# Backward pass of an attention block on one core: dW4 computed at the turn from the forward to the backward part, and two tiles used a second time

## The chip, the core and the metric

The kernel runs on one core of a Trainium2 chip. A core has TensorE (PE: matrix products into PSUM), VectorE (DVE), ScalarE (ACT), GpSimd (POOL) and SyncE (SP), each with an instruction queue of its own, and 16 DMA engines that move data between the chip's large memory (HBM) and the on-chip SBUF. Here SP issues almost all loads and POOL all stores. The metric is device time in microseconds, lower is better; a run without the profiler gives one time, and the kernel before is given by the median of three.

## What is computed

One token goes through a decoder block with a modulated layer norm, attention over a cache of 8192 positions for 32 heads of width 192, and a small MLP; wanted are the output and the gradients towards nine of the inputs. Cut to what matters here:

```python
def _A_ref(x, k_cache, v_cache, wq, wo):              # attention, one query row
    scores = jnp.einsum('bhqd,bhkd->bhqk', q, k) * Dh ** (-0.5)
    p = _softmax(scores, axis=-1)
    o = jnp.einsum('bhqk,bhkd->bhqd', p, v)
    return o.reshape(B, Sq, Hq * Dh) @ wo
def _fwd_reference(...):
    x = x + ga * _A_ref(h, A_k_cache, A_v_cache, A_wq, A_wo)
    h = _layernorm(x) * (1 + cb) + sb
    x = x + gb * _B_ref(h, B_w1, B_w2, B_w3, B_w4)    # ... gelu(layernorm(.) @ w3) @ w4
...
_out, _vjp = jax.vjp(_f, A_x, A_k_cache, A_v_cache, A_wq, A_wo, B_w3, B_w4, c, w_mod)
```

With a single token, every weight's gradient is an outer product of two vectors. For W4 (1536 x 640) it is the activation g = gelu(u), 1536 long, times the gradient at the MLP's output, 640 long: dW4[f, :] = g[f] * dbo[:]. For the V cache, dV of a head is the softmax row p times the gradient do of that head's output (8192 x 192), and dK is the same with dS and q. All data is bfloat16. K and V are read (V twice), dK and dV are written: about 100 MB each.

## The kernel before

**Forward part.** A loop over 32 heads streams K and V in half heads of 128 partitions x 32 rows x 192 (`JH` = 32; 1.5 MB each), forms scores, softmax and the products with V. The normalised exponentials (`E_all`) stay on chip.

**The turn.** After the last head, the rest of the forward part and the start of the backward part run as one chain of small steps in a column layout (a vector of 1536 lies as 128 x 12, its columns called f): layer norms, u = n2 W3, gelu, g (`g_f` in float32, `g_bf`), then du, dn2 = W3 du, two layer norm backward steps (`ln_bwd_cols`, "lb2" and "lb1"), dao, do of the last head pair (`do_bf`, spread over the partitions as `do_pb`). W3 and W4 sit in three of the five 1.5 MB tiles of the pool `big`: `w_t[0]` holds the first 512 rows of W3, `w_t[1]` the last 128 rows of W3 and 7 of 12 blocks of W4, `w_t[2]` the other 5 blocks of W4 and a rest of the transposed W3; a fourth, `w_t[3]`, holds the transposed W3, written block by block (`w3T_some`) and read by the dn2 matmuls (L764). `mid_mm` (matmuls of L798) computes g W4 from `w_t[1]` and `w_t[2]`. The fifth tile of the pool holds half of V of head 30.

`ln_bwd_cols` has a `fill` callback that is called between the matmul for the means and VectorE's use of its result. For "lb2" it transposes two blocks of wo (`woT_some(2)`), for "lb1" it is `lb1_fill` (one more block, the broadcast of q, and a copy).

**Backward part.** A loop over the heads from the last to the first (`HS`). For a head, `bwd_mult` multiplies V by do on VectorE and sums over the width on TensorE; `bwd_dv` makes dV for half a head: ScalarE makes the first `na` = 20 of 32 row blocks (L903), VectorE the other 12 (L880, `pairs_outer`), and POOL issues the store (L909). `bwd_ds` and `bwd_dk` make dK on VectorE, stored by L924. dV and dK take their tiles from `big`, in the order in which the pool's tiles come free. For the very first half (`bwd_dv(HS[0], 0, 0, 2)`) VectorE makes all 32 row blocks, in two pieces, each with its own store. V comes through a ring of six tiles and is loaded ahead as far as the ring allows.

Gradients of the weights are jobs attached to the heads of the loop (`J0`, `J1`, `J2`): `job_dwo` at heads 1 to 16, `job_dw4` at 17 to 20, `job_dw3` at 21 to 25, and larger jobs for wq and w_mod. `job_dw4(k)` makes three of twelve row blocks on ScalarE (`tsc` with k even, L939) in a tile of the pool `bso` (two tiles) and stores them with one DMA (L947). `job_dw3` multiplies on VectorE (L941).

The order of TensorE, VectorE and ScalarE is the order in which the instructions are written (`pin_order`); POOL's and SP's queues are ordered by the framework's scheduler, and all waits between engines are set by the framework from the tiles that are read and written.

Of the kernel before, what the change touches and what calls it, by code (L numbers as in the profile page):

```python
# [9 lines left out]
BF16 = mybir.dt.bfloat16  # L10
ALU = mybir.AluOpType
# [9 lines left out]
def kernel(  # L21
# [26 lines left out]
    nc = tc.nc  # L48
# [16 lines left out]
    P = 128  # L65
    D = A_x.shape[-1]
    _, HQ, S, DH = A_k_cache.shape
# [10 lines left out]
    HH = HQ // 2  # L78
# [6 lines left out]
    NAV = 40  # L85
# [8 lines left out]
    def bank(tag, bufs=1, name=None, n=512):  # L94
        return psum[0].tile([P, n], FP32, tag=tag, name=name or "ps_" + tag, bufs=bufs)
# [31 lines left out]
    def ccol(n, name, dtype=FP32):  # L127
        return const.tile([P, n], dtype, name=name)

    def mul(out, a, b):  # L130
        nc.vector.tensor_tensor(out=out, in0=a, in1=b, op=ALU.mult)  # L131

    def add(out, a, b):
        nc.vector.tensor_tensor(out=out, in0=a, in1=b, op=ALU.add)  # L134
# [4 lines left out]
    def stt(out, in0, scalar, in1, op0, op1):  # L139
        nc.vector.scalar_tensor_tensor(out=out, in0=in0, scalar=scalar, in1=in1, op0=op0, op1=op1)  # L140
# [6 lines left out]
    def neg_means(parts, n, name):  # L147
        ps = bank_c(name)
        nc.tensor.matmul(ps[:, 0:n], lhsT=negd_mat, rhs=parts, start=True, stop=True)
        return ps[:, 0:n]  # L150

    def ln_cols(x_c, pfx, fill=lambda k: None):
        s1 = ccol(1, pfx + "_s1")
        nc.vector.reduce_sum(out=s1, in_=x_c, axis=AX.X)
        m_ps = neg_means(s1, 1, pfx + "_m")
        fill(0)
        xc = ccol(NDC, pfx + "_xc")
        add(xc, x_c, m_ps.to_broadcast([P, NDC]))
        sq = ccol(NDC, pfx + "_sq")
        s2 = ccol(1, pfx + "_s2")  # L160
        nc.vector.tensor_tensor_reduce(out=sq, in0=xc, in1=xc, scale=1.0 / D, scalar=0.0, op0=ALU.mult, op1=ALU.add, accum_out=s2)
        v_ps = col_sums(s2, 1, pfx + "_v")
        std = ccol(1, pfx + "_std")
        nc.scalar.activation(out=std, in_=v_ps, func=ACT.Sqrt, bias=eps_c[:, 0:1], scale=1.0)
        rstd = ccol(1, pfx + "_rstd")
        nc.vector.reciprocal(out=rstd, in_=std)
        fill(1)
        nrm = ccol(NDC, pfx + "_n")
        nc.vector.tensor_scalar(out=nrm, in0=xc, scalar1=rstd[:, 0:1], scalar2=None, op0=ALU.mult)
        return nrm, rstd  # L170

    def ln_bwd_cols(dn, n, rstd, add_to, out, pfx, fill=lambda: None):
        s = ccol(2, pfx + "_s")
        nc.vector.reduce_sum(out=s[:, 0:1], in_=dn, axis=AX.X)
        jk = ccol(NDC, pfx + "_jk")
        nc.vector.tensor_tensor_reduce(out=jk, in0=dn, in1=n, scale=1.0, scalar=0.0, op0=ALU.mult, op1=ALU.add, accum_out=s[:, 1:2])
        m_ps = neg_means(s, 2, pfx + "_m")
        fill()
        t = ccol(NDC, pfx + "_t")
        mul(t, n, m_ps[:, 1:2].to_broadcast([P, NDC]))  # L180
        add(t, t, dn)
        add(t, t, m_ps[:, 0:1].to_broadcast([P, NDC]))
        stt(out, t, rstd[:, 0:1], add_to, ALU.mult, ALU.add)

    def bcast_cols(col_bf, c0, n, out_bc, evac, ps_in=None):
        for g0 in range(0, n, 4):
            g1 = min(n, g0 + 4)
            ps = ps_in if ps_in is not None else bank_c("bc_ps")
            for k in range(g0, g1):
                nc.tensor.matmul(ps[:, (k - g0) * P : (k - g0 + 1) * P], lhsT=col_bf[:, c0 + k : c0 + k + 1].to_broadcast([P, P]), rhs=ident_bf, start=True, stop=True)  # L190
            evac(out_bc[:, g0 * P : g1 * P], ps[:, 0 : (g1 - g0) * P])
# [4 lines left out]
    def dve_copy(out, in_):  # L196
        nc.vector.tensor_copy(out=out, in_=in_)
# [26 lines left out]
    def big_tile(name):  # L224
        return big.tile([P, JH, DH], BF16, name=name, tag="big")
# [84 lines left out]
    dbo_c = ccol(NDC, "dbo_c")  # L310
# [3 lines left out]
    dbo_bc = const.tile([P, D], BF16, name="dbo_bc")  # L314
# [24 lines left out]
    def pair_bc(pool, col_bf, hp, name, ps=None):  # L339
        t = pool.tile([P, 2 * DH], BF16, name=name, tag=name)  # L340
        bcast_cols(col_bf, 3 * hp, 3, t, act_copy, ps)
        return t
# [152 lines left out]
    def flat(tl):  # L495
        return tl.rearrange("p j d -> p (j d)")
# [48 lines left out]
    for i in range(1, HQ + 2):  # L545
        if i == HQ + 1:
            nc.scalar.activation(out=warm, in_=eps_c, func=ACT.Sqrt)
        c, p, pp = 2 <= i < HQ, 0 <= i - 1 < HQ, 0 <= i - 2 < HQ
        n = i + 1 < HQ
# [5 lines left out]
        if i == HQ - 1:  # L555
            w_t = [flat(big_tile(f"w_t{k}")) for k in range(2)]
# [78 lines left out]
    def woT_some(n):  # L635
        for g in range(woT_next[0], min(woT_next[0] + n, 4)):
            t_ps = bank("s", 2, "t_ps", SB[0])
            blks = range(4 * g, min(4 * g + 4, 3 * NDC))
            for k, blk in enumerate(blks):
                nc.tensor.matmul(t_ps[:, k * P : (k + 1) * P], lhsT=woT[:, blk * P : (blk + 1) * P], rhs=ident_bf, start=True, stop=True)  # L640
            nc.scalar.copy(out=woT[:, 512 * g : 512 * g + P * len(blks)], in_=t_ps[:, 0 : P * len(blks)])
        woT_next[0] += n
# [20 lines left out]
    bso = ctx.enter_context(tc.tile_pool(name="bso", bufs=2, reuse_waits="tile"))  # L663
    bsm = ctx.enter_context(tc.tile_pool(name="bsmall", bufs=2, reuse_waits="tile"))
    HS = list(range(HQ - 1, -1, -1))
# [35 lines left out]
    st2 = nc.gpsimd  # L701
# [27 lines left out]
    n2_c, r2 = ln_cols(hb_c, "ln2", lambda k: w3T_some(k + 1))  # L729
# [27 lines left out]
    g_f = ccol(NFC, "g_f")  # L757
    mul(g_f, u, sg)
    g_bf = ccol(NFC, "g_bf", BF16)
    dve_copy(g_bf, g_f)  # L760
    dn2_ps = bank("b")
    for i in range(NDC):
        for f in range(NFC):
# [3 lines left out]
    dn2 = ccol(NDC, "dn2")  # L767
    dve_copy(dn2, dn2_ps[:, 0:NDC])
    dhb = ccol(NDC, "dhb")
    ln_bwd_cols(dn2, n2_c, r2, dbo_c, dhb, "lb2", lambda: woT_some(2))  # L770
    def lb1_fill():
        woT_some(1)
        q_pb[PS[0]] = pair_bc(bsm, q_bf, PS[0], "q_pb")
        nc.scalar.copy(out=kb_sb, in_=kb_ps[:, 0 : 2 * DH])

    dn1 = ccol(NDC, "dn1")
    mul(dn1, dhb, cb1)
    dx1 = ccol(NDC, "dx1")
    ln_bwd_cols(dn1, n1_c, r1, dy_c, dx1, "lb1", lb1_fill)
    dao_bf = ccol(NDC, "dao_bf", BF16)  # L780
    mul(dao_bf, dx1, ga)
# [104 lines left out]
    def vec_of(d, h):  # L886
        return d[h // 2][:, (h % 2) * DH : (h % 2 + 1) * DH]
# [7 lines left out]
            nc.tensor.matmul(bst[h]["dP_ps"][:, t * JH : (t + 1) * JH, :], lhsT=ident_bf, rhs=V_sb[:, :, k * DS : (k + 1) * DS], start=(k == 0), stop=(k == NDS - 1))  # L895
        freed.add(("v", h, t))

    def bwd_dv(h, t, na=NAV // 2, parts=1):
        o = big_tile("dV")
        j0 = t * JH  # L900
        doh = vec_of(do_pb, h)
        for jj in range(na):
            nc.scalar.activation(out=o[:, jj, :], in_=doh, func=ACT.Copy, scale=bst[h]["PF"][:, j0 + jj : j0 + jj + 1])  # L903
        n = JH // parts
        for r0 in range(0, JH, n):
            r1 = r0 + n
            ra = max(r0, na)
            pairs_outer(o[:, ra:r1, :], bst[h]["P2h"][:, j0 + ra : j0 + r1, :], doh, r1 - ra)
            st2.dma_start(out=dV_hd[h][:, j0 + r0 : j0 + r1, :], in_=o[:, r0:r1, :])  # L909
# [27 lines left out]
    def tsc(out, in_, col, k):  # L937
        if k % 2 == 0:
            nc.scalar.activation(out=out, in_=in_, func=ACT.Copy, scale=col)  # L939
        else:  # L940
            nc.vector.tensor_scalar(out=out, in0=in_, scalar1=col, scalar2=None, op0=ALU.mult)  # L941

    def job_dw4(k):
        o = bso.tile([P, 3, D], BF16, name="dw4", tag="so")
        for cc in range(3):
            tsc(o[:, cc, :], dbo_bc, g_f[:, 3 * k + cc : 3 * k + cc + 1], 0)
        st2.dma_start(out=out_7[3 * k * P : 3 * (k + 1) * P, :].rearrange("(c p) r -> p c r", p=P), in_=o)  # L947

    def job_dw3(i):
        o = bso.tile([P, F], BF16, name="dw3", tag="so")  # L950
        tsc(o, du_bc, n2_c[:, i : i + 1], 1)
        st2.dma_start(out=out_6[i * P : (i + 1) * P, :], in_=o)
# [66 lines left out]
    J0, J1, J2 = [{i: [] for i in range(HQ)} for _ in range(3)]  # L1019
    for k in range(HH):  # L1020
        J1[1 + k].append(lambda hp=PS[k]: job_dwo(hp))
    for k in range(4):
        J1[1 + HH + k].append(lambda k=k: job_dw4(k))
    for k in range(NDC):
        J1[5 + HH + k].append(lambda i=k: job_dw3(i))

    def add_outer(at, name, view, lo, n, col_bf, rows_f, dram, acc, first):
        J2[at].append(lambda: job_outer_load(name, view, lo, n))
# [16 lines left out]
    for b, ks in enumerate(BATCHES):  # L1045
        units = [(PS[k], cc) for k in ks for cc in range(3)]
        i = 1 + 2 * b
# [23 lines left out]
    for cc in range(3):  # L1071
        for j in range(NDC):
            blk = cc * NDC + j
            nc.tensor.matmul(do_ps[:, cc : cc + 1], lhsT=woT[:, blk * P : (blk + 1) * P], rhs=dao_bf[:, j : j + 1], start=(j == 0), stop=(j == NDC - 1))
    dve_copy(do_bf[:, 3 * PS[0] : 3 * PS[0] + 3], do_ps[:, 0:3])
    do_pb[PS[0]] = pair_bc(bsm, do_bf, PS[0], "do_pb")
    bcast_dao()
    mid_mm()
    bwd_dv(HS[0], 0, 0, 2)
    c_first = fin_c(PS[0], 1)  # L1080
    bwd_dv(HS[0], 1)
    AHEAD = 2 * NPH
    for i in range(HQ):
        h, nxt = HS[i], HS[i + 1] if i + 1 < HQ else None
# [73 lines left out]
```

## Time and profile before

| | us |
|---|---|
| median of 3 runs (lowest, highest) | 1394.95 (1394.62, 1397.5) |
| the profiled execution, its own time | 1396.62 |
| its span, first to last instruction | 1394.8 |
| busy: PE, DVE, ACT, POOL | 856.1, 1078.9, 964.2, 114.9 |
| moved by DMA | 570.81 MB, mean 409 GB/s |
| stretch of the turn at a DMA share of 0.04 | 574 to 584 |
| dW4's ScalarE work | 1043.1 to 1124.4, 12 instructions, 9.0 in all |
| dW4's four stores, issue to landing | 16.5 to 31.6 |

The span is shorter than the time that the same execution took, by 1.8 us that lie before the first and after the last recorded instruction. Busy time of an engine is an average over parts with different limits; which engine waits for which in a stretch is read from the rows of that stretch. The chain that ended last is listed from its end backwards and alternates, from 1188 us on, between VectorE's work and dV stores that take 23 to 32 us to land; the last such wait ends at 1327 us.

### The profile page before, as it was taken

To read this page: it belongs to the slowest core of one execution; us is meant where nothing else is said; L and a number is where in the kernel's file an instruction comes from. 1 tells how busy PE (TensorE), PEld (TensorE's weight loads), DVE (VectorE), ACT (ScalarE), POOL (GpSimd) and SP (SyncE) were. 2 spreads that over 40 slices of the span, in tenths; PEclk is the share of its full clock that TensorE was granted. 3 is DMA by queue.
4 is the path that set the end of the run, shared out by engine and by line. 5 is a ranking of instruction groups with operands and counts; after the bars stand their busy time and mean duration, and the time that the engine had idled before them with its cause. 6 is when DMAs were issued, how large, how long until landed. Compare 5 with 4: busy or idle time off the path is not lost. (4 is left out here: it accounts for less than half of the span.)

```text
span 1394.8 us, 28118 instructions
## 1 busy us (share of the span) xinstructions
PE 856.1 (61%) x11519; PEld 672.9 (48%) x11519; DVE 1078.9 (77%) x1276; ACT 964.2 (69%) x2633; POOL 114.9 (8%) x207
## 2 busy tenths in 40 slices
PE   3699999999999999737635642443432435323342
PEld 3577777777777777626525541322222223212231
DVE  3588878878888886699988984975768659666796
ACT  1487778877777787786795586566766766566582
POOL 0000000000000000011101110211111111111011
PEclk9799999999999999666656665666675666755666
DMA  9999999999999999699999999999999999999988
GB/s 392 418 420 417 415 410 416 418 404 402 418 412 408 413 417 403 241 384 397 426 427 425 425 428 427 427 427 427 427 427 424 424 424 419 426 409 416 407 352 367
DMA packets 71711, 570.81 MB, mean 409 GB/s; under 512 B 6878, under 2 KB 18398, under 8 KB 31134
## 3 DMA queue, kind: packets, MB, share of 16 engines
q1 hardware_dynamic: 46496, 339.16, 59.2%
q0 software_dynamic: 25056, 229.85, 39.1%
q8 instruction: 90, 1.47, 0.4%
q14 instruction: 39, 0.32, 0.1%
q10 hardware_dynamic: 30, 0.00, 0.0%
HBM read 343.08 MB, written 225.91 MB: 408 GB/s over the span
## 5 line engine op out<-in xcount | busy, mean ns | idle before, releaser
L903 ACT ACTIVATE dV<-do_pb,PF 128x192 bf16<-128x192 bf16 x1260 | 439.3, 440 | 90.9 <-DMA out_dram<-dK 60.6
L895 PE MATMUL dP_ps<-V_sb,ident_bf 128*128 128x256 bf16 x1536 | 232.1, 326 | 258.6 <-DVE V_sb L131 258.6
L391 ACT ACTIVATE EK<-K_sb,E_f 128x192 bf16<-128x192 bf16 x1024 | 364.5, 442 | 22.1 <-PE kb_ps L432 14.0
L895 PEld LDWEIGHTS <-ident_bf 128*128 128x128 bf16 x1536 | 179.4, 117 | 311.0 <-issue 177.9
L880 DVE TENSOR_TENSOR dK<-dS,q_pb 128x6144 bf16<-128x6144 bf16 (+1 forms) x67 | 213.2, 3211 | 47.0 <-DMA out_dram<-dK 43.2
L131 DVE TENSOR_TENSOR prod<-K_sb,q_pb 128x6144 bf16<-128x6144 bf16 x64 | 214.6, 3354 | 23.5 <-DMA K_sb<-in_A_k_cache_dram 18.0
L131 DVE TENSOR_TENSOR V_sb<-V_sb,do_pb 128x6144 bf16<-128x6144 bf16 x64 | 211.8, 3350 | 6.6 <-DMA V_sb<-in_A_v_cache_dram 6.6
L416 PE MATMUL ps_a<-EK,V_sb 128*128 128x193 bf16 x2048 | 202.1, 252 | 3.1 <-DMA V_sb<-in_A_v_cache_dram 2.3
L416 PEld LDWEIGHTS <-V_sb 128*128 128x128 bf16 x2048 | 175.6, 100 | 21.8 <-issue 17.4
L880 DVE TENSOR_TENSOR dV<-P2h,do_pb 128x2304 bf16<-128x2304 bf16 (+1 forms) x65 | 87.2, 1368 | 56.1 <-DMA out_dram<-dV 44.0
L399 DVE TENSOR_TENSOR EK<-K_sb,P2h 128x1536 bf16<-128x1536 bf16 x128 | 121.6, 950 | 0.0
L424 PE MATMUL ps_b<-EK,V_sb 128*64 128x193 bf16 x2048 | 110.8, 250 | 8.2 <-DVE MB_all L134 7.9
L359 PE MATMUL S_ps<-prod,ident_bf 64*64 64x256 bf16 x3072 | 99.7, 277 | 7.2 <-DVE prod L131 7.2
L424 PEld LDWEIGHTS <-V_sb 128*64 128x64 bf16 x2048 | 84.4, 109 | 28.9 <-issue 28.7
L359 PEld LDWEIGHTS <-ident_bf 64*64 64x64 bf16 x3072 | 82.3, 109 | 22.8 <-issue 22.3
L380 ACT ACTIVATE E_f<-sm_ps,negm 128x64 f32<-128x64 f32 x32 | 10.1, 315 | 104.9 <-DVE negm L378 104.9
L909 POOL DMA_DIRECT2D out_dram<-dV x65 | 34.8, 535 | 462.6 <-ACT dV L903 313.7
L432 PE MATMUL kb_ps<-EK,hot_bf 128*32 128x384 bf16 x1024 | 65.9, 335 | 2.0 <-DVE q_bf L304 2.0
L981 PEld LDWEIGHTS <-ident_bf 128*128 128x128 bf16 x112 | 14.5, 130 | 91.4 <-issue 88.9
L194 ACT CAST do_pb<-bc_ps 128x384 bf16<-128x384 f32 x16 | 7.5, 470 | 69.0 <-PE bc_ps L190 69.0
L939 ACT ACTIVATE wq_o<-wq_bc,ha_f 128x1536 bf16<-128x1536 bf16 x12 | 18.5, 1565 | 47.8 <-DMA out_dram<-wq_o 47.8
L924 POOL DMA_DIRECT2D out_dram<-dK x67 | 37.1, 554 | 165.0 <-DVE dK L880 126.5
(249 smaller groups left out, 821.8 us busy)
## 6 DMA issues: line engine op xcount, KB each, us to landing
V_sb<-in_A_v_cache_dram SPq DMA_DIRECT2D x126, 1536.0 KB, 11.8
K_sb<-in_A_k_cache_dram SPq DMA_DIRECT2D x64, 1536.0 KB, 13.7
out_dram<-dV POOLq DMA_DIRECT2D x63, 1536.0 KB, 18.5
out_dram<-dK POOLq DMA_DIRECT2D x63, 1536.0 KB, 20.8
wq<-in_A_wq_dram SPq DMA_DIRECT2D x3, 2560.0 KB, 33.9
wo_t<-in_A_wo_dram SPq DMA_DIRECT2D x16, 480.0 KB, 12.4
out_dram<-dwo POOLq DMA_DIRECT2D x16, 480.0 KB, 19.5
wq<-in_A_wq_dram SPq DMA_DIRECT2D x4, 1920.0 KB, 29.7
```

The lines of the kernel that those rows point to most:

```text
L131: nc.vector.tensor_tensor(out=out, in0=a, in1=b, op=ALU.mult)
L359: nc.tensor.matmul(st["S_ps"][c0 : c0 + 64, r, t * JH : (t + 1) * JH, :], lhsT=ident_bf[64 * r : 64 * r + 64, 64 * r : 64 * r + 64], rhs=p ...
L391: nc.scalar.activation(out=EK[:, jj, 0:DH], in_=K_st[h, t][:, r * JQ + jj, :], func=ACT.Copy, scale=st["E_f"][:, j : j + 1])
L399: nc.vector.tensor_tensor(out=EK[:, NA:JQ, 0:DH].rearrange("p j (d r) -> p j d r", r=2), in0=K_st[h, t][:, r * JQ + NA : (r + 1) * JQ, :]. ...
L416: nc.tensor.matmul(st["A_ps"][:, 0 : DH + 1], lhsT=V_sb[:, r * JQ + jj, a0:a1], rhs=EK[:, jj, 0 : DH + 1], start=(q == 0 and jj == 0), sto ...
L424: nc.tensor.matmul(st["B_ps"][g : g + 64, 0 : DH + 1], lhsT=V_sb[:, r * JQ + jj, b0:b1], rhs=EK[:, jj, 0 : DH + 1], start=(q == 0 and jj < ...
L432: nc.tensor.matmul(kb_ps[g : g + 32, 0 : 2 * DH], lhsT=hot_bf[:, HQ - 1 - h : 2 * HQ - 1 - h], rhs=EK[:, jj : jj + 2, 0:DH], start=(h == 0 ...
L880: nc.vector.tensor_tensor(out=o.rearrange("p j (d r) -> p j d r", r=2), in0=pairs[:, :, None, :].to_broadcast([P, n, NP2, 2]), in1=vec.rea ...
L895: nc.tensor.matmul(bst[h]["dP_ps"][:, t * JH : (t + 1) * JH, :], lhsT=ident_bf, rhs=V_sb[:, :, k * DS : (k + 1) * DS], start=(k == 0), sto ...
L903: nc.scalar.activation(out=o[:, jj, :], in_=doh, func=ACT.Copy, scale=bst[h]["PF"][:, j0 + jj : j0 + jj + 1])
L909: st2.dma_start(out=dV_hd[h][:, j0 + r0 : j0 + r1, :], in_=o[:, r0:r1, :])
L924: st2.dma_start(out=dK_hd[h][:, j0 : j0 + n, :], in_=o[:, r0 : r0 + n, :])
```

## The change

dW4 is no longer a job of four heads of the backward loop. Its twelve row blocks are multiplied by VectorE at the turn: six as soon as g is there (ahead of the copy of dn2), two in the `fill` of "lb2", two in that of "lb1", two after `do_bf`. Blocks 0 to 8 are written into `w_t[0]`, whose W3 rows have by then been read for the last time; blocks 9 to 11 into a tile of `bso`. Three stores of 6, 3 and 3 blocks are issued after blocks 5, 8 and 11. The jobs for dW3 move up by four heads. The first half of dV of the last head is written into `w_t[3]` instead of a new tile of `big`.

```diff
@@ -758,6 +758,19 @@
     g_bf = ccol(NFC, "g_bf", BF16)
     dve_copy(g_bf, g_f)
+    dw4_last = bso.tile([P, 3, D], BF16, name="dw4_last", tag="so").rearrange("p c r -> p (c r)")
+    dw4_n = [0]
+
+    def dw4_some(n):
+        for f in range(dw4_n[0], dw4_n[0] + n):
+            tl, c0 = (w_t[0], 0) if f < 9 else (dw4_last, 9)
+            nc.vector.tensor_scalar(out=tl[:, (f - c0) * D : (f - c0 + 1) * D], in0=dbo_bc, scalar1=g_f[:, f : f + 1], scalar2=None, op0=ALU.mult)
+            if f in (5, 8, 11):
+                f0 = 0 if f == 5 else f - 2
+                st2.dma_start(out=out_7[f0 * P : (f + 1) * P, :].rearrange("(c p) r -> p c r", p=P), in_=tl[:, (f0 - c0) * D : (f + 1 - c0) * D].rearrange("p (c r) -> p c r", r=D))
+        dw4_n[0] += n
+
+    dw4_some(6)
     dn2_ps = bank("b")
...
-    ln_bwd_cols(dn2, n2_c, r2, dbo_c, dhb, "lb2", lambda: woT_some(2))
+
+    def lb2_fill():
+        woT_some(2)
+        dw4_some(2)
+
+    ln_bwd_cols(dn2, n2_c, r2, dbo_c, dhb, "lb2", lb2_fill)
+
     def lb1_fill():
         woT_some(1)
+        dw4_some(2)
...
-    def bwd_dv(h, t, na=NAV // 2, parts=1):
-        o = big_tile("dV")
+    def bwd_dv(h, t, na=NAV // 2, parts=1, o=None):
+        o = big_tile("dV") if o is None else o
...
-    def job_dw4(k):
-        o = bso.tile([P, 3, D], BF16, name="dw4", tag="so")
-        for cc in range(3):
-            tsc(o[:, cc, :], dbo_bc, g_f[:, 3 * k + cc : 3 * k + cc + 1], 0)
-        st2.dma_start(out=out_7[3 * k * P : 3 * (k + 1) * P, :].rearrange("(c p) r -> p c r", p=P), in_=o)
...
-    for k in range(4):
-        J1[1 + HH + k].append(lambda k=k: job_dw4(k))
     for k in range(NDC):
-        J1[5 + HH + k].append(lambda i=k: job_dw3(i))
+        J1[1 + HH + k].append(lambda i=k: job_dw3(i))
...
     dve_copy(do_bf[:, 3 * PS[0] : 3 * PS[0] + 3], do_ps[:, 0:3])
+    dw4_some(2)
     do_pb[PS[0]] = pair_bc(bsm, do_bf, PS[0], "do_pb")
     bcast_dao()
     mid_mm()
-    bwd_dv(HS[0], 0, 0, 2)
+    bwd_dv(HS[0], 0, 0, 2, w_t[3].rearrange("p (j d) -> p j d", d=DH))
     c_first = fin_c(PS[0], 1)
```

On POOL's queue the three stores stand ahead of all dV stores, and the first dK store of the last head now stands ahead of the second dV store of the head after it; from there on the queue's order is as before, apart from dW4 and dW3. TensorE's and SP's instructions are unchanged.

## The prediction, made before the changed kernel had run

> **What bounds the kernel now.** I read the page's slices first, then the busy time by stretch, then the turn in order of time, then the groups by line.
>
> ```profile
> DVE  3588878878888886699988984975768659666796
> DMA  9999999999999999699999999999999999999988
> GB/s 392 418 420 417 415 410 416 418 404 402 418 412 408 413 417 403 241 384 397 426 427 425 425 428 427 427 427 427 427 427 424 424 424 419 426 409 416 407 352 367
> ```
>
> Each digit is a tenth of a slice of 34.9 us. The 16 DMA engines are full in all slices but three: the seventeenth (558 to 593 us, the turn from the forward to the backward part, 241 GB/s) and the last two. So the time is bytes over rate plus the stretches in which the DMA has nothing to do. The columns below: stretch, length, busy us and count of PE, PEld, DVE, ACT, POOL, then granted clock, DMA share, GB/s.
>
> ```profile
> 563.00:574.00 11.00, 9.57 (x163) 7.96 (x161) 4.01 (x26) 8.64 (x17) 0.00 (x0) 0.62 0.83 320
> 574.00:584.00 10.00, 8.56 (x137) 7.63 (x134) 6.02 (x21) 6.98 (x18) 0.56 (x1) 0.50 0.04 13
> 588.00:590.00 2.00, 0.65 (x4) 0.45 (x4) 2.00 (x2) 1.97 (x7) 0.53 (x1) 0.50 0.23 98
> 593.00:597.00 4.00, 3.46 (x32) 2.85 (x30) 4.00 (x7) 4.00 (x13) 0.53 (x1) 1.00 0.61 178
> 640.00:700.00 60.00, 43.73 (x265) 38.23 (x263) 59.13 (x80) 37.73 (x99) 8.28 (x14) 0.65 1.01 417
> 700.00:1240.00 540.00, 220.70 (x1355) 163.56 (x1353) 402.43 (x331) 364.39 (x926) 76.34 (x133) 0.65 1.01 426
> 1240.00:1300.00 60.00, 21.53 (x142) 16.12 (x140) 45.10 (x31) 35.55 (x99) 6.93 (x13) 0.67 0.99 399
> ```
>
> From 574 to 584 the DMA share is 0.04: the V loads fill every free buffer by 574, and no store is ready before dV of the last head. From 700 to 1240 the DMA share is 1.01 while VectorE is busy 402 of 540 us and ScalarE 364: there the DMA alone sets the pace. In the turn a chain of tiny steps sets it:
>
> ```profile
> 572.23 0.17 DVE L197 CAST g_bf<-g_f 128x12 bf16<-128x12 f32 x1
> 572.60 2.03 PE L764 MATMUL ps_b<-du_bf,w_t 128*128 128x1 bf16 x60
> 574.67 0.17 DVE L197 COPY dn<-ps_b 128x5 f32<-128x5 f32 x1 [2.27 <-PE ps_b L764]
> 575.79 0.16 DVE L131 TENSOR_TENSOR lb_t<-ln_n,lb_m 128x5 f32<-128x5 f32 x1 [0.68 <-PE lb_m L149]
> 577.75 0.16 DVE L131 TENSOR_TENSOR lb_t<-ln_n,lb_m 128x5 f32<-128x5 f32 x1 [0.68 <-PE lb_m L149]
> 580.68 3.43 DVE L880 TENSOR_TENSOR dV<-P2h,do_pb 128x3072 bf16<-128x3072 bf16 x2 [1.11 <-ACT do_pb L194]
> 580.75 1.79 PE L798 MATMUL h_ps<-g_bf,w_t 128*128 128x1 bf16 x60
> 581.23 7.02 ACT L903 ACTIVATE dV<-do_pb,PF 128x192 bf16<-128x192 bf16 x20
> 582.74 0.56 POOL L909 DMA_DIRECT2D out_dram<-dV  x1 [42.10 <-DVE dV L880]
> ```
>
> The brackets are VectorE's idle time before the row: 2.27, 0.68, 0.68 and 1.11 us of waiting, and POOL issues nothing for 42.10 us before the first dV store.
>
> **dW4 leaves the full stretch.**
>
> ```profile
> L939 ACT ACTIVATE dw<-dbo_bc,g_f 128x640 bf16<-128x640 bf16 x12 | 9.0, 812 | 0.0
> L941 DVE TENSOR_SCALAR dw<-du_bc,ln_n 128x1536 bf16<-128x1536 bf16 x5 | 3.1, 614 | 0.0
> L941 DVE TENSOR_SCALAR wm_o<-wm_bc,sc_f 128x1280 bf16<-128x1280 bf16 x6 | 3.3, 547 | 0.0
> ```
>
> Twelve ScalarE multiplications of 0.81 us (1043 to 1125 us) and four stores of 480 KB go from heads 17 to 20 of the backward loop; the five dW3 jobs move up from heads 21 to 25 into 17 to 21, so the bytes are missing from 21 to 25. ScalarE's 9.0 us are worth nothing there: it is 67% busy. The bytes are: 4 x 480 KB = 1.966 MB, at the 426 GB/s of 700 to 1240, 4.6 us. Lower bound of this term: 0, if that stretch is held by something else than DMA; upper bound: rows of 1280 bytes may move slower than the mean. The nearest row for that is the load of wo in the same row length, 350 GB/s between 560 and 563, which makes 5.6 us. I take 4.6, since the 88 us with dW4 in them ran at 424 against 426 to 427 around them.
>
> **dW4 arrives in the turn.** VectorE multiplies in its waits. A 128x640 multiplication by a column has no row; from 614 ns for 1536 columns and 547 for 1280 it is 0.26 ns per column, so 0.38 us, of which neighbours overlap some 0.08 (the two 3.35 us V products take 6.62). Six of them behind g_bf: 572.4 to about 574.3, before the copy of dn at 574.67; two in each of the 0.68 us waits take 0.68, just filling them; two between do_bf (579.56) and dV (580.68) end at 580.2. The first six wait for the last transposes that read W3's tile (done at 572.81), which doesn't push them past 574.67 by more than 0.1. I charge 0.1 us in all. Without any cover it would be 12 x 0.38 = 4.6 us on this chain, which is what dV, the V products and every later store follow.
>
> The three stores go first on POOL's queue, ahead of the dV stores. Their issue costs 0.76 us (three chunks, the row of dwo), up to 0.95 (the load of seven chunks at 533 us). Ready at 574.3, 577.5 and 580.2, data flowing about a microsecond after issue begins (dV: issue 582.74, data from 583.8): 0.98, 0.49 and 0.49 MB in 2.3, 1.15 and 1.15 us, so roughly 575.7 to 578.0, 579 to 580, 581.6 to 582.8. All lies in the empty 574 to 583.8, and POOL is free at 581.3, before dV's first issue at 582.74. Cost 0; without that cover they would push dV back by up to 4.6 us, and the gain would be nil. V loads are not behind them: SP's next load is at 593.87, when its buffer comes free.
>
> POOL's issues meet VectorE's multiplications: at 1108.17 a dK issue that overlaps a multiplication took 0.76 us where it takes 0.53 elsewhere. The Trainium skill (SBUF — State Buffer, Who interferes with whom) says that multiplications by a column can take a port pair shared with GpSimd's descriptor writing, and that the one that comes second blocks wholly. By that rule the first store's issue (574.6 to 575.5) holds the seventh and eighth multiplication back by some 0.5 us, and the sum below would be 3.8 in place of 4.3; the row shows only the issue stretched, by 0.23 us, and I don't charge it.
>
> **dV of the last head into W3's transposed tile.** The first half, two VectorE pieces of 128x3072, is written in place: the tile's last readers are the matmuls that end at 574.63, so no wait, as before. But dV's tiles now rotate differently. The second half of dV took that tile before and began at 581.23; now it gets the tile of W3's last rows and W4, which the 60 matmuls of L798 read until 582.54. ScalarE begins near 582.6, 1.4 us later, its 7.0 us end at 589.6 instead of 588.25, and the store of 1.5 MB follows. Behind it on ScalarE stand the next two dV (13.93 us) and do_pb at 602.36, which the V product at 606.29 needs: 2.1 us of slack remain (do_pb then ends near 604.2), and the dV after it waited 4.6 us for a store anyway. The DMA is empty 1.4 us longer before that store, but the store then fills the gaps of 593 to 597 (share 0.61, 1.6 us empty). I charge 0.2, bounds 0 and 1.4. The next head's second dV now waits for the dW4 stores in W3's tile (landed by 584, needed at 597): 0. On POOL the first dK goes ahead of that dV store: dK ready at 603.0, dV at 603.8, so that order is the one in which they finish.
>
> **Sum.** -4.6 + 0.1 + 0.2 = -4.3 us, bounds -5.6 and, with nothing covered, -4.6 + 4.6 + 1.4 = +1.4. The profiled span of 1394.8 us becomes 1390.5; that execution took 1396.62, 1.8 more than its span, and the median of the runs is 1394.95. From the median: 1390.6, with 1389 to 1392 as the range of this case alone.
>
> **Rivals.**
> 1. *Bytes were hidden anyway* (18%). If what is saved at heads 21 to 25 turns into waiting elsewhere, the end hardly moves. For it: VectorE is busy 59.1 of 60 us in 640 to 700, and 17.9 of 18 us in 1342 to 1360 with DMA share 0.75, so both ends of the backward part are VectorE's; from 1240 to 1300 the rate drops to 399. Against it: 540 us in between at share 1.01, and the last long wait of the chain that ended last, until 1327, is for a dV store to land. A fixed tail only shifts. It would give 0 to -2.8, about 1393.5.
> 2. *The turn comes late* (12%). The chain from g_bf to dV pays for the multiplications. Price: nothing covered, 4.6; three issues that block VectorE, 0.76 + 0.76 + 0.95 = 2.5; ScalarE 1.4: 8.5 in all, less 4.6, is +3.9, about 1398.9. It decides once dV's first half starts more than 4.3 us late, beyond 585.0. For it: the two 0.68 us waits have no room left. Against: the other two have 0.4 and 0.5, and each overrun is tenths.
> 3. *The late dips close* (6%). At 399 against 426 GB/s, 1240 to 1300 loses 3.8 us, and 1342 to 1360, at 311, 4.9. Without dW3 in heads 22 to 25 VectorE and POOL are a little lighter there; if half of this went, 4.3 us, the time would be about 1386.3. The five tiles of dV and dK rotate as before from the third head on, so I see no reason for it.
> That the change doesn't do what it says (dW4's stores held back in the queue until dV's) would show as rival 1 and is in its 18%.
>
> **Numbers.** Forecast 64%, rivals 18, 12 and 6. Two runs of this kernel differ by up to 0.2% (1394.62 to 1397.5), 2.8 us, which is what a measurement can tell. Faster by more than that: the forecast and rival 3, 0.70; within: rival 1, 0.18; slower: rival 2, 0.12. The range, 1387.2 to 1396.5, leaves out part of rivals 2 and 3.
>
> **What would show it.** Right: 574 to 584 with a DMA share near 0.45 instead of 0.04; dV's first half within 0.5 us of 580.68; ScalarE's first dV piece waiting for L798's line until about 582.6; the DMA share at 1.01 from 700 on, the last heads earlier by 4 us. Wrong: multiplications longer than 0.4 us, dn's copy later than 574.9, a V product that waits for do_pb at 606, or a share below 1 in 1100 to 1240.

## The result, and the profile after

The changed kernel took 1388.59 us (1388.47 to 1389.18, 4 runs) beside 1395.76 (4 runs) of the kernel before: ratio 0.9948, 95% interval 0.9931 to 0.9966, or 7.2 us less. Run a second time, beside the experiments below, it took 1390.89 us (1388.13 to 1393.84, 11 runs) beside 1395.30 (23 runs): ratio 0.9972, interval 0.9962 to 0.9981, or 4.4 us less by the medians (3.9 by the ratio). The forecast, 4.3 us less (ratio 0.9969), lies in the second interval and just outside the first; of the two medians, the second lies in the 1389 to 1392 us that the prediction gave as the range of this case alone, the first 0.4 us below it. Where the first pair's extra 2.9 us come from is a question of its own below.

The slices of the changed kernel's page, span 1386.6 us:

```profile
DMA  9999999999999999799999999999999999999998
GB/s 391 418 412 415 418 418 405 420 419 407 420 409 412 413 416 405 283 389 398 428 426 425 425 429 428 427 428 428 426 424 420 427 423 412 427 417 413 420 385 361
```

The seventeenth slice now moves 283 GB/s instead of 241. Busy time by stretch, columns as in the prediction (DMA share and GB/s last):

```profile
563.00:574.00 11.00, 9.90 (x178) 8.44 (x175) 5.49 (x29) 8.02 (x16) 0.16 (x1) 0.56 0.76 297
574.00:584.00 10.00, 8.57 (x122) 7.57 (x119) 8.37 (x31) 6.46 (x17) 2.77 (x4) 0.50 0.63 233
588.00:590.00 2.00, 1.28 (x7) 0.88 (x7) 2.00 (x2) 1.97 (x7) 0.53 (x1) 0.50 0.04 8
593.00:597.00 4.00, 2.54 (x24) 2.02 (x21) 4.00 (x8) 4.00 (x13) 0.53 (x1) 1.00 1.02 349
640.00:700.00 60.00, 44.12 (x259) 38.42 (x260) 59.13 (x78) 37.72 (x100) 7.74 (x13) 0.64 1.01 418
700.00:1240.00 540.00, 228.40 (x1390) 168.42 (x1389) 409.22 (x338) 355.69 (x914) 73.59 (x130) 0.66 1.01 425
1240.00:1300.00 60.00, 15.00 (x106) 11.53 (x104) 38.80 (x25) 41.90 (x118) 6.91 (x13) 0.62 1.01 419
```

The empty ten microseconds from 574 to 584 now carry 2.3 MB (share 0.63, before 0.04). The gap around 588 to 590 is deeper than before (0.04, before 0.23), and the one of 593 to 597 is gone (1.02, before 0.61). From 640 to 1240 the DMA's share and rate are the same to within 1 GB/s. The turn in order of time:

```profile
571.60 0.17 DVE L197 CAST g_bf<-g_f 128x12 bf16<-128x12 f32 x1
571.68 1.86 DVE L767 TENSOR_SCALAR w_t<-dbo_bc,g_f 128x640 bf16<-128x640 bf16 x6
573.84 0.84 POOL L770 DMA_DIRECT2D out_dram<-w_t  x1 [34.65 <-DVE w_t L767]
574.05 0.17 DVE L197 COPY dn<-ps_b 128x5 f32<-128x5 f32 x1 [0.51 <-PE ps_b L777]
574.40 0.69 DVE L767 TENSOR_SCALAR w_t<-dbo_bc,g_f 128x640 bf16<-128x640 bf16 x2
575.16 0.16 DVE L131 TENSOR_TENSOR lb_t<-ln_n,lb_m 128x5 f32<-128x5 f32 x1
577.13 0.16 DVE L131 TENSOR_TENSOR lb_t<-ln_n,lb_m 128x5 f32<-128x5 f32 x1
580.04 3.43 DVE L900 TENSOR_TENSOR w_t<-P2h,do_pb 128x3072 bf16<-128x3072 bf16 x2 [0.52 <-ACT do_pb L194]
580.12 1.79 PE L818 MATMUL h_ps<-g_bf,w_t 128*128 128x1 bf16 x60
581.86 7.02 ACT L923 ACTIVATE dV<-do_pb,PF 128x192 bf16<-128x192 bf16 x20 [1.15 <-issue]
589.17 0.53 POOL L929 DMA_DIRECT2D out_dram<-dV  x1 [4.57 <-ACT PF L711]
```

In this execution the forward part ended 0.63 us sooner, so times are compared from g_bf on. From there to dV's first half it took 8.45 us before (572.23 to 580.68) and takes 8.44 now. The waits in brackets have shrunk from 2.27 to 0.51, from 0.68 to nothing (twice) and from 1.11 to 0.52: the multiplications stand in them. ScalarE's dV piece starts 10.26 us behind g_bf, where it was 9.00: 1.26 us later, with an idle time of 1.15 us before it. The view names no releaser for that wait ("issue"); it ends when the 60 matmuls of L818, which read W4, end (580.12 + 1.79 = 581.91).

**Where the time went.** For each stretch I take its length times (1 - rate / 427 GB/s): the time that the DMA lost there. All four rows move the same bytes; rates are whole GB/s, so the long stretches are good to a microsecond. The second row of each kernel is the second profile taken with the experiments.

| | span | 0 to 574 | 574 to 601 | 601 to 1240 | 1240 to the end |
|---|---|---|---|---|---|
| before | 1394.8 | 24.2 | 15.1 | 3.9 | 14.9 |
| before, again | 1396.0 | 26.9 | 14.4 | 5.4 | 12.8 |
| changed | 1386.6 | 24.2 | 9.5 | 5.6 | 10.6 |
| changed, again | 1388.1 | 24.2 | 9.9 | 5.4 | 11.4 |

The turn lost 14 to 15 us and loses 9.5 to 9.9: about 5 us are gained there, in both pairs. The four turns begin up to 3.4 us apart (`g_bf` starts at 572.23, 575.04, 571.60 and 572.99), so that fixed stretches cut them at different places. Over 27 us counted from 1.77 us behind the start of `g_bf` (574 to 601 in the first profile), the loss is 15.1 and 15.4 us before and 10.0 and 10.2 changed: 5.1 us in both pairs. These 27 us are called the turn's account below. The other stretches scatter by 1 to 3 us between two profiles of the same kernel. In the first pair the last stretch gave another 4.3 us; in the second, 1.4.

### The profile page after: what moved, and what is told of

Its sections match the earlier page's. It is cut to its first block, busy times and chain, and to the rows that moved or that the text cites. A ratio compares the mean times of both kernels' runs of the same rounds, so it can differ in the third digit from the quotient of the medians.

```text
span 1386.6 us, 28120 instructions
## 1 busy us (share of the span) xinstructions
PE 859.9 (62%) x11519; PEld 675.5 (49%) x11519; DVE 1082.2 (78%) x1288; ACT 955.7 (69%) x2621; POOL 114.0 (8%) x206
## 4 chain that ended last, share of the span: by engine, by line
DMA 46%; DVE 26%; PE 15%; issue 8%; ACT 3%; another core or an unknown queue 1%; POOL 1%; POOLq 0%; ACTq 0%; DVEq 0%; SPq 0%
DMA out_dram<-dV 18%; DMA K_sb<-in_A_k_cache_dram 13%; DMA out_dram<-dK 6%; DVE prod L131 6%; DVE V_sb L131 5%; PE ps_a L416 5%; DVE dK L900 4%; DMA V_sb<-in_A_wo_dram 3%; DMA V_sb<-in_A_v_cache_dram 3%; PE ps_b L424 2%; DMA out_dram<-wq_o 2%; PE S_ps L359 2%; ACT EK L391 2%; DVE dV L900 2%; DVE S L363 2%
## 5 line engine op out<-in xcount | busy, mean ns | idle before, releaser
L391 ACT ACTIVATE EK<-K_sb,E_f 128x192 bf16<-128x192 bf16 x1024 | 364.6, 442 | 23.1 <-PE kb_ps L432 14.1
L900 DVE TENSOR_TENSOR dV<-P2h,do_pb 128x2304 bf16<-128x2304 bf16 x63 | 83.9, 1356 | 47.5 <-DMA out_dram<-dV 44.1
L995 PEld LDWEIGHTS <-ident_bf 128*128 128x128 bf16 x112 | 14.9, 133 | 84.9 <-issue 82.5
L397 DVE CAST EK<-E_f 128x16 bf16<-128x16 f32 x128 | 25.4, 198 | 33.7 <-PE kb_ps L432 27.8
```

Of the source, the lines that this page charges most:

```text
L391: nc.scalar.activation(out=EK[:, jj, 0:DH], in_=K_st[h, t][:, r * JQ + jj, :], func=ACT.Copy, scale=st["E_f"][:, j : j + 1])
L900: nc.vector.tensor_tensor(out=o.rearrange("p j (d r) -> p j d r", r=2), in0=pairs[:, :, None, :].to_broadcast([P, n, NP2, 2]), in1=vec.rea ...
```

## The experiments

Three theories stood for what the first pair had gained beyond dW4's bytes: A, dW3's leaving heads 22 to 25; B, dW4's leaving ScalarE and POOL; C, the scatter of the late loop.

**dW3 where it was.** One line of the changed kernel is undone.

```diff
-        J1[1 + HH + k].append(lambda i=k: job_dw3(i))
+        J1[5 + HH + k].append(lambda i=k: job_dw3(i))
```

> The changed kernel with one line undone: the five dW3 jobs stay at heads 21 to 25. The changed kernel took 7.2 us less than the one before, of which 4.6 us are dW4's bytes moved into the empty turn; the windows put the rest into the stretch from 1240 us to the end. Theory A (dW3's leaving heads 22 to 25 closes the late dips): about 1391.3, 4.4 below before, and the dips of 1240 to 1300 back at about 400 GB/s. Theory B (dW4's leaving ScalarE and POOL at heads 17 to 20 does it): as the changed kernel, 1388.6. Theory C (the late loop falls into a different rhythm with any shift of the work): anywhere between 1387 and 1392, with dips at other places than before.

Measured: 1389.36 us (1387.59 to 1390.49, 6 runs) beside 1395.13 (21 runs), ratio 0.9951, interval 0.9936 to 0.9966. Theory A wanted the late dips back and 1391.3; the stretch from 1240 to 1300 ran at 415 GB/s, and the time is below. A is not supported.

**dW4 left out, and dW3 late or early.** Both leave dW4's output unwritten; the turn is that of the kernel before.

```diff
-    for k in range(4):
-        J1[1 + HH + k].append(lambda k=k: job_dw4(k))
```

> The kernel before with dW4 left out altogether (that output is not written), dW3 at heads 21 to 25 as before, the turn as before. It shows what 1.966 MB less in the full stretch is worth without anything done at the turn. Theory A: 4.6 us less than before, 1391.2. Theory B: the same 7.2 as the changed kernel, 1388.6, as ScalarE and POOL lose their jobs here too. Theory C: somewhere from 1387 to 1392.

> As the run without dW4 (its output is not written), but with the dW3 jobs moved up to heads 17 to 21 as in the changed kernel. The turn is as before, with nothing multiplied or stored early. Theory A: 1388.3, 3 us below the run without dW4 alone. Theory B: equal to it. If the turn's early stores cost nothing, as forecast, this run and the changed kernel (1388.6) agree to 0.5 us; a lower time here is what the turn pays, the 1.2 us of ScalarE's wait and more.

Measured: dW3 late 1389.68 us (1385.5 to 1394.05, 10 runs), ratio 0.9952, interval 0.9937 to 0.9967; dW3 early 1390.80 us (1388.7 to 1392.18, 6 runs), ratio 0.9960, interval 0.9944 to 0.9976. A wanted the second 3 us below the first; it is 1.1 above, and the intervals overlap. Not having dW4 in the loop at all is worth 5.5 and 4.3 us by the medians (intervals 4.6 to 8.8 and 3.3 to 7.8), which is about what the changed kernel gains in its two measurements. That doesn't tell B from C: either run alone would fit both, and what speaks for C is that one program ranges over 8.6 us.

**Only the second part of the change.**

```diff
-    bwd_dv(HS[0], 0, 0, 2)
+    bwd_dv(HS[0], 0, 0, 2, w_t[3].rearrange("p (j d) -> p j d", d=DH))
```

> The kernel before with only the second part of the change: the first half of dV of the last head goes into the tile of the transposed W3, dW4 stays a job at heads 17 to 20. The second half of dV then gets the tile of W3's first rows, free since 572.8, so ScalarE does not wait. All theories: no change, 1395.8 within 1 us. If the order of the tiles matters for the late rhythm (theory C), up to 3 us either way.

Measured: 1395.88 us (12 runs) beside 1395.13, ratio 1.0006, interval 0.9994 to 1.0019, so -0.8 to +2.7 us: no change that could be told, and the gain comes with dW4's move. ScalarE's dV piece starts 9.01 us behind `g_bf` here, as in the kernel before (9.00): the second part alone does not make ScalarE wait.

**The changed kernel again.**

> The changed kernel unaltered, a second time, beside the runs that follow. The first four runs agreed within 0.7 us at 1388.6 while the kernel before has so far ranged from 1392.5 to 1400.1. If the part of the gain above 4.6 us is the late rhythm of one execution (theory C), this run's median comes nearer to 1390 with a spread of several us; if it is a steady property of the changed kernel, 1388.6 within 1 us.

Measured: 1390.89 us, a spread of 5.7 us over 11 runs, ratio 0.9972. The 0.7 us of the first four runs was not the kernel's real spread, and 1388.6 was its good side. Of the theories, C is the one that expected this.

**The turn's work on top of the old jobs.** dW4 is made and stored twice, at the turn and by the four jobs.

```diff
+    for k in range(4):
+        J1[1 + HH + k].append(lambda k=k: job_dw4(k))
     for k in range(NDC):
-        J1[1 + HH + k].append(lambda i=k: job_dw3(i))
+        J1[5 + HH + k].append(lambda i=k: job_dw3(i))
```

> The changed kernel, with dW4 made and stored a second time by the four old jobs at heads 17 to 20 and dW3 back at heads 21 to 25. The late loop then carries what it carried before, and the turn carries its new work on top. If the turn's work is free (forecast: 0.1 + 0.2 us), the time is that of the kernel before, 1395.1, within 1 us. If the turn pays 1.2 us or more for ScalarE's wait or for the multiplications, 1396.5 or more. If the early stores help by more than their bytes, for instance by starting the stores sooner, below 1394.

Measured: 1394.98 us (12 runs) beside 1395.30, ratio 1.0006, interval 0.9993 to 1.0018. The turn's work and its 1.97 MB are free within that interval, whose upper end is 2.5 us. In this profile `g_bf` starts at 574.25, 2.65 us later than in the changed kernel's, so its turn is read 2.65 us later too. It carries what 574 to 584 carries in the changed kernel (share 0.63, 233 GB/s), the turn's account is 10.2 us, and the gain is gone as soon as the loop has its bytes back:

```profile
576.65:586.65 10.00, 8.57 (x122) 7.56 (x119) 8.38 (x31) 6.47 (x17) 2.79 (x4) 0.50 0.63 233
```

**What the bytes cost in the full stretch.** Each of dW4's four stores in the kernel before is followed by three of the same size, in rows of 1280 bytes, or in rows of 3840.

```diff
+        for m in range(3):
+            n3 = 3 * P * D
+            a = ((3 * k + m) % 6) * n3
+            flat_dk = out_2[0, (3 * k + m) // 6].rearrange("s d -> (s d)")[a : a + n3]
+            st2.dma_start(out=flat_dk.rearrange("(c p r) -> p c r", p=P, r=D), in_=o)
```

The second has `"(p c r) -> p c r"` in the last line.

> The kernel before, with each of dW4's four stores followed by three more of the same 480 KB in rows of 1280 bytes, into rows of dK of the first two heads that are written over at the end. It adds 5.9 MB in the full stretch and nothing else. At the 426 GB/s that the forecast used: 13.8 us, 1408.9. If rows of 1280 bytes move at 350 GB/s, as next to the load of wo: 16.9 us, 1412. The price of dW4's own 1.97 MB is a third of what is measured: 4.6 by the first, 5.6 by the second.

> As the run before it, but the three added stores lay the same 480 KB out as 3840 bytes in a row for each partition. If the row length matters, this adds less: 13.8 us against 16.9. If not, both add the same, 13.8 within 1.5.

Measured, beside 1395.30: 1414.62 us (4 runs), ratio 1.0138, interval 1.0125 to 1.0151, so 19.3 us; and 1410.43 us (4 runs), ratio 1.0111, interval 1.0098 to 1.0124, so 15.1 us. The first is above both figures that were expected for it (13.8 and 16.9), the second 1.3 us above its 13.8. A third of it is 6.4 us in rows of 1280 bytes and 5.0 in rows of 3840. The stretch from 1000 to 1200 in the kernel before, with the narrow rows and with the wide ones:

```profile
1000.00:1200.00 200.00, 77.69 (x502) 56.15 (x502) 143.61 (x97) 137.62 (x347) 30.59 (x54) 0.67 1.01 424
```

```profile
1000.00:1200.00 200.00, 75.12 (x484) 54.98 (x483) 138.09 (x94) 126.02 (x317) 36.88 (x62) 0.66 1.00 412
```

```profile
1000.00:1200.00 200.00, 77.82 (x489) 55.67 (x487) 140.01 (x93) 124.71 (x314) 34.80 (x62) 0.67 1.01 419
```

At the same DMA share of 1.0 the rate falls from 424 to 412 and 419 GB/s: the engines are as busy and move less. But 6.4 us is the price of a burst of four stores, and the stores' own packets take less. The traces record every DMA packet with its size and its time. A store in rows of 1280 bytes moves in packets of 5120 bytes, four rows each. The 1152 packets added here took 201 ns each, 14.5 us in all (the sum of their times over 16 engines), the 768 packets of 7680 bytes of the wide rows 293 ns each, 14.1 us. So of the 4.2 us between the spans of the two profiles the row length itself explains 0.4. All other packets together took 1.3 us longer with the narrow rows, and the time in which the engines moved nothing was 2.5 us longer. Why is open.

What dW4 itself costs in the full stretch can be read from its 384 packets. From 1040 to 1170 the kernel before has 704 packets of 5120 bytes and the changed kernel 320. They took 8.70 and 4.02 us in the first pair of profiles, 8.64 and 3.93 in the second, so dW4's took 4.7 us, about 196 ns each. In the changed kernel's turn the same 384 packets took 5.4 us, 224 ns each or 365 GB/s over 16 engines. A row of that stretch, in which no other load or store is in flight:

```profile
576.00:578.00 2.00, 1.25 (x8) 1.09 (x9) 1.73 (x11) 1.21 (x4) 0.77 (x1) 0.50 0.94 335
```

335 GB/s at a share of 0.94 is 356 at full share. So the same stores move more slowly alone in the turn than in the mixed traffic of the loop, and their price there is not the price here.

**All twelve multiplications in one block.**

```diff
-    dw4_some(6)
+    dw4_some(12)
```

The three later calls go.

> The changed kernel with all twelve multiplications in one block behind g, ahead of the copy of dn. Twelve at a pitch of 0.30 us take 3.6 us where the wait for dn is 2.3: the chain up to dV's first half comes about 1.2 us late, measured from g's end, while the stores come earlier. The tiles then rotate otherwise (the second half of dV waits for dW4's stores instead of the matmuls of L798). If the turn's chain sets the pace of all that follows, as the forecast had it, 1.2 us slower than the changed kernel at 1390.9: 1392.1. If the turn's chain has slack, 1390.9.

```profile
570.88 2.75 DVE L767 TENSOR_SCALAR w_t<-dbo_bc,g_f 128x640 bf16<-128x640 bf16 x9
573.54 0.97 DVE L767 TENSOR_SCALAR dw_last<-dbo_bc,g_f 128x640 bf16<-128x640 bf16 x3
580.43 1.76 DVE L898 TENSOR_TENSOR w_t<-P2h,do_pb 128x3072 bf16<-128x3072 bf16 x1 [1.11 <-ACT do_pb L194]
```

From g_bf (570.79) to dV it took 9.64 us instead of 8.44: the chain pays 1.2 us, as worked out. The time was 1391.83 us (11 runs) beside 1395.87, ratio 0.9971, interval 0.9959 to 0.9983; the changed kernel's was 0.9972. The trace shows the lateness, the time can't tell 1.2 us from none. The turn's account does: it is 11.8 us here, 1.6 to 1.8 more than in the changed kernel's two profiles.

POOL's first issue shows something that the changed kernel doesn't show. It began while VectorE was multiplying (until 574.51) and took 1.88 us, where the same issue took 0.84 in the changed kernel:

```profile
573.04 1.88 POOL L770 DMA_DIRECT2D out_dram<-w_t  x1 [34.12 <-DVE w_t L767]
```

**Filling the gap before 590.** dV's second half of the last head is stored in four parts (`bwd_dv(HS[0], 1, parts=4)`, with VectorE's piece left out of parts that are all ScalarE's); then its first half in four pieces too.

> The changed kernel with the second half of dV of the last head stored in four parts of eight row blocks instead of one. In the changed kernel the DMA is empty from 587.2 to 590, until ScalarE has finished 20 row blocks; here the first part is ready after eight, near 584.7. If an empty stretch of the turn is worth its length wherever it is filled, 2 to 2.8 us less than the changed kernel: 1388.5 beside 1390.9. If the stretch around 590 is VectorE's, not the DMA's (VectorE is busy 98% from 584 to 700), no change.

> As the run before it, and the first half of dV in four pieces instead of two, so that its first store starts some 0.9 us sooner, into the gap near 582.5. Same reasoning: up to 0.8 us less than the run before it, 1387.8; VectorE pays two more instruction starts, about 0.1 us.

The stretch from 587 to 590 in the changed kernel and with the parts:

```profile
587.00:590.00 3.00, 1.28 (x7) 0.88 (x7) 3.00 (x2) 2.97 (x10) 0.53 (x1) 0.50 0.10 32
```

```profile
587.00:590.00 3.00, 1.73 (x9) 1.23 (x9) 3.00 (x2) 2.97 (x9) 1.61 (x3) 0.50 0.66 262
```

The gap is filled (share 0.10 to 0.66). The times: 1390.03 us (12 runs), ratio 0.9962, interval 0.9950 to 0.9975; and 1391.61 us (5 runs), ratio 0.9966, interval 0.9954 to 0.9978. Both overlap with the changed kernel's 0.9972 (0.9962 to 0.9981). The turn's account is 9.9 and 10.4 us, the changed kernel's 10.0 and 10.2: what now moves in the gap is missing elsewhere in the same 27 us. Neither is shown to be better than the changed kernel.

**The kernel before again**, for a second profile.

> The kernel before, unaltered, for a second profile. Theory C says that what the DMA loses after 1240 us (14.9 us of time at 427 GB/s in the first profile, 10.6 in the changed kernel's) differs between executions of one program by several us: here some other figure than 14.9, and the span moves with it. If 14.9 is a property of the kernel before, it comes again within 1 us.

One run, 1397.82 us, span 1396.0. Its last stretch lost 12.8 us, not 14.9: 2.1 us apart in one and the same program. From 1240 to 1300 it ran nearly as slowly as in the first profile, though (402 against 399), while from 1300 to 1342 it was better (422 against 414):

```profile
1240.00:1300.00 60.00, 23.27 (x157) 17.55 (x155) 44.97 (x29) 33.85 (x94) 8.09 (x16) 0.67 0.99 402
1300.00:1342.00 42.00, 14.61 (x102) 11.41 (x102) 31.59 (x17) 26.99 (x79) 4.19 (x8) 0.64 1.00 422
```

So the sum of the dips is partly the execution's; and dips from 1240 to 1300 come without dW4 in the loop too (393 GB/s in the run with all twelve in one block, 407 in the one without dW4 and with dW3 early). Over all twelve profiles but the two with the fourfold stores (two of each kernel and eight of the variants) the last stretch lost between 9.1 and 14.9 us: 12.4 to 14.9 in the four with dW4 in the loop, 9.1 to 13.1 in the eight without. A small systematic part in it, a microsecond or two in favour of a loop without dW4, is not excluded; B and C are not told apart to that degree. The same shows from the start of `g_bf` to the end of the span, which leaves the forward part out: 820.9 to 822.5 us in the four, 815.0 to 815.1 in the changed kernel's two and the one with dW3 late, 813.1 to 818.9 over all eight. The turn's account is 14.9 to 15.9 us in the seven profiles with nothing of dW4 at the turn and 9.9 to 10.4 in the six with the multiplications in the waits.

## Why the prediction was right, point by point

- **The DMA sets the pace from 700 to 1240, so bytes taken out there are worth their time.** Right. Leaving dW4 out entirely gains about what the changed kernel gains; adding the bytes back with the turn unchanged takes all of it away; adding three times as much in that stretch costs 15 to 19 us.
- **The size of that term, 4.6 us.** Right as far as it can be measured: dW4's packets took 4.7 us in the full stretch, and the turn's account fell by 5.1. Whether other transfers also ran faster once these packets were gone is not resolved. The upper bound of 5.6 came from the load of wo, which was not the nearest row: that load moves in packets of one row of 1280 bytes (55 to 58 ns each, some 360 GB/s), these stores in packets of four. The 6.4 us of the added stores is not this term's price either: with a turn that is free it would be the whole gain, and the second measurement's interval is 2.7 to 5.3 us. The reason given for 4.6, 424 against 426 to 427 GB/s around it, was weak: only a few per cent of the bytes there are dW4's.
- **What a measurement can tell, 2.8 us.** Too small. It was taken from three runs of the kernel before; 21 runs of it ranged over 7.6 us. That the sum of -4.3 agrees with the second measurement's -4.4 to 0.1 us is luck: that measurement's interval is 2.6 us wide, and terms of 0.1 and 0.2 can't be tested by the time.
- **VectorE's multiplications fit into its waits, 0.1 us.** Right, with 0.0 measured on the chain. The wait for the last transposes, which the forecast put ahead of the first six, isn't seen: they began 0.08 us behind the start of `g_bf`, while L631's transposes still ran. The duration worked out from two longer rows, 0.38 us, is what the group shows:

```profile
L767 DVE TENSOR_SCALAR w_t<-dbo_bc,g_f 128x640 bf16<-128x640 bf16 x9 | 2.9, 383 | 0.0
```

- **POOL's issues against the multiplications.** The rule of the Trainium skill (SBUF — State Buffer, Who interferes with whom) would have held the seventh and eighth back by some 0.5 us. The first store's issue ran from 573.84 to 574.68, the two began at 574.40 and took 0.69 us together, the pitch of the others, and lb_t followed without idle time. Here the trace doesn't show the block on VectorE's side, and the 0.5 us by which 3.8 differs from 4.3 was not lost; but the two met for only the last 0.28 us of the issue. On POOL's side something like it is seen in the run with all twelve multiplications together, where an issue that began during them took 1.88 us in place of 0.84.
- **The stores land in the empty stretch.** Right: the share from 574 to 584 is 0.63. The forecast said 0.45, for 4.6 us of transfers; dW4's packets took 5.4 there, and the rest is dV's first store, whose data begin inside these ten microseconds. dV's first store was still issued at 582.10, as far behind g_bf as before (10.50 us, before 10.51).
- **ScalarE waits for the matmuls that read W4, 1.4 us, of which 0.2 are paid.** The wait is 1.26 us, and the matmuls of L818 (L798 before) end with it, though the view doesn't name them; the gap of 588 to 590 is deeper, and that of 593 to 597 is filled, as worked out. That hardly anything is paid agrees with the run that has the turn's work on top of the old jobs (interval -1.0 to +2.5 us); 0.2 itself is below what it can tell.
- **The rivals.** That the bytes were hidden anyway fell: its price was at most 2.8 us, and leaving dW4 out gains 4.6 to 8.8 (with dW3 early 3.3 to 7.8). By the changed kernel's own time alone it would be close, since the second interval begins at 2.7. The late turn fell: dV's first half is not late. The closing of the late dips, which was given 6%, is seen in the first pair of profiles (399 to 419 GB/s in 1240 to 1300), where the stretch from 1240 to the end gave 4.3 of the 8.2 us between the spans; in the second pair it gave 1.4. Its cause as the rival had it, dW3's leaving heads 22 to 25, was tried and not supported. That it also makes the 7.2 us of the first four runs is likely and not shown, and what causes it is open.

## What to carry to other kernels

Where one resource is full for most of the time, look for the stretch in which it stands still, and move work of that resource there; what it is worth is the price of the same work in the full stretch, and it costs nothing as long as the chain that ends the empty stretch keeps its length, which the trace shows to a hundredth of a microsecond. Price a store by its own packets in the traffic that it leaves: neither a load with the same row length, nor the same rows moving alone, nor a burst of four times as many gave that price here. Line up the executions at the same instruction before comparing stretches of the turn. And where a closed loop of buffers and queues runs for hundreds of microseconds, four runs that agree within 0.7 us are no measure of the spread: repeat both kernels before explaining the last 3 us.

## What the hardware showed that was not expected

- Stores in rows of 1280 bytes took about 196 ns for a packet of 5120 bytes in the mixed traffic of the loop (some 418 GB/s over 16 engines) and 224 ns (365 GB/s) alone in the turn. Fourfold in the full stretch, 5.9 MB of them cost 19.3 us, against 15.1 us in rows of 3840 bytes (intervals 17.4 to 21.1 and 13.7 to 17.3), of which the packets themselves explain 14.5 and 14.1. Part of the rest may be POOL's queue, on which four stores in a row hold up the dK stores behind them; that wasn't separated.
- A store's issue on POOL that began while VectorE was multiplying by columns without a pause took 1.88 us instead of 0.84; multiplications that began during the last 0.28 us of such an issue kept their pitch.
- One program's runs ranged over 5.7 us (changed kernel, 11 runs), 7.6 us (before, 21 runs) and 8.6 us (without dW4, 10 runs), though in the two kernels' profiles the time from `g_bf` to dV's first half agrees to a few hundredths of a microsecond. `g_bf` itself started between 570.67 and 575.04 us in the fourteen profiles, and the stretch from 1240 to the end lost 9.1 to 14.9 us in twelve of them: the scatter is seen in the long streaming parts.
